# Gate projection of four token groups, in place of two, by seven block products

## The chip, the cores and the metric

The kernel runs on one core of one Trainium2 chip. The metric is the device time of one execution in microseconds (us), as the median of several executions. An engine is named as the profile names it: PE (TensorE, matrix products), DVE (VectorE), ACT (ScalarE), POOL (GpSimd) and SP (SyncE, which issues transfers). A bank is one of the eight parts of the matmul accumulator memory, 128 x 512 float32 each.

## The reference

Linear attention with cosine and sine weights, and behind it a gated feed-forward block. There are 8 batches with 8 heads of 576 positions of 64, which make 4608 tokens of 512; the hidden size is 1536.

```python
def phi(x, c, s):
    r = np.maximum(x, 0.0)
    return np.concatenate([r * c, r * s], axis=-1)
q_p = phi(q, cos_w, sin_w)
k_p = phi(k, cos_w, sin_w)
kv = np.einsum('bhsf,bhsd->bhfd', k_p, v)
z = np.sum(k_p, axis=2)
num = np.einsum('bhsf,bhfd->bhsd', q_p, kv)
den = np.einsum('bhsf,bhf->bhs', q_p, z)[..., None] + 1e-06
x = num / den                      # then heads side by side: (4608, 512)
...
g = x @ w_gate
silu = g * (1.0 / (1.0 + np.exp(-g)))
val = x @ w_val
return (silu * val @ w_out).astype(np.float32)
```

## The kernel before

**Groups and tiles.** The 4608 tokens are worked on in nine groups (0 to 8) of 512 tokens. A group has four tiles of 128 tokens. A tile comes out of the attention part as x (eight small matmuls on PE at line 435, then den, rec and x on DVE at lines 445, 454 and 458), and its transpose xT is made by a DMA transpose that SP issues (line 535). A batch has 576 tokens, so some tiles span two batches and take 16 matmuls.

**A group's feed-forward.** In the plain form (`ffn_fc`, line 571) a group takes twelve steps. In each, PE makes the gate and the value projection of 128 hidden columns, with four matmuls of 512 columns each (line 551); ACT takes silu of the gate (557) and DVE multiplies both into ht (562). Then the output projection follows (`out_by_quarters`, line 754, for groups 2 to 8), which already uses seven block products for eight; its operands are the weight differences T1 to T4 and the sums S1 to S4 of ht (line 747, `token_sum`).

**The seven-product form of the gate.** Groups in the tuple `GATE` use `ffn_by_quarters` (line 594) instead. The gate product of a third of the hidden columns (index u, three thirds) is seen as a 2 x 2 product of blocks: gate weights A11 to A22, tokens by depth B11 to B22. Seven products of four matmuls of 256 columns each (line 608) take the place of eight. The sums of weights W1 to W4 are made once (`gate_weight_sum`, 584), the differences of tokens X1 to X4 once for each group (`x_sum`, 592). Two intermediate results are copied by ACT (636 seeds bank b from bank a; 640 copies a product to m7), and two are added by DVE (646: c = m7 + b; 655: m7 = m7 + b) before four silus (614) read a, m7, c and b. The value projections V stay as they are (620), placed between the products, and the multiplication into ht is at line 625.

**The banks.** `take` (line 78) hands out banks by what was used longest ago. It prefers, for the banks of this form, a bank whose neighbour is in use, as long as fewer than three whole pairs are free, because a tile and a key-value product need a whole pair. In the first third of group 7 the second V is so given the bank that a had, which a silu has just read, and the third V the bank that c had.

**Order.** The program of each engine is in the order in which the lines are called. The dictionary `plan` holds what is done behind each step ("slot"): a group has 16 slots, twelve in its feed-forward (in the seven-product form the twelve calls of `done`) and four in its output projection. Into these slots go the tiles of the next group, the preparation of the next batch (q: relu on ACT at 253 and DVE products r_q at 270, DMA transposes phit at 293; k and v: relu at 253, DVE products at 274; key-value product on PE at 320 in slot 5 with its copies on ACT and DVE at 343), and the sums above. In groups 5 and 6 slots 0 to 2 hold three of the four k and v preparations of the next batch, and slot 5 its key-value product. Group 7 and 8 have neither.

**What depends on `GATE`.** Line 1021 spreads the four weight sums over slot 15 of groups between 1 and `GATE[0]`; line 1024 puts the four x differences of a group into slots 14 and 15 of the group before; line 1039 gives the slots of the tiles made in a group of `GATE`; lines 1044 to 1049 choose the form.

Of the kernel before, what the change touches and what calls it, by code (L numbers as in the profile page):

```python
# [18 lines left out]
def kernel(  # L19
# [29 lines left out]
    HT = T // 2  # L49
    HD = d_model // 2  # L50
    KH = KC // 2
    GATE = (7, 8)

    consts = ctx.enter_context(tc.tile_pool(name="consts", bufs=1))
    raw = ctx.enter_context(tc.tile_pool(name="raw", bufs=2))
# [515 lines left out]
    def ffn_fc(*a):  # L571

        ffn_mm(*a)
        ffn_act(*a)
# [6 lines left out]
    def gate_weight_sum(n):  # L581
        o, x, y, op = ((W1, A21, A22, ALU.add), (W2, W1, A11, ALU.subtract), (W3, A11, A21, ALU.subtract),
                       (W4, A12, W2, ALU.subtract))[n]
        nc.vector.tensor_tensor(out=o, in0=x, in1=y, op=op)
# [278 lines left out]
    def at(s, *fns):  # L863
        plan.setdefault(s, []).extend(fns)

    def slot(s):
        for f in plan.pop(s, ()):
            f()
# [151 lines left out]
    for n in range(4):  # L1020
        at(SLOTS * (1 + n * (GATE[0] - 1) // 4) + FC + 3, lambda n=n: gate_weight_sum(n))
    for tg in GATE:
        for n in range(4):
            at(SLOTS * (tg - 1) + FC + (2, 2, 3, 3)[n], lambda tg=tg, n=(2, 0, 1, 3)[n]: x_sum(tg, n))
    for t in range(2 * OUT, NTG * OUT):
# [9 lines left out]
        else:  # L1035
            if t in (13, 14, 15):
                s = SLOTS * 2 + t - 4
            elif tg - 1 in GATE:
                s = SLOTS * (tg - 1) + ((1, 2, 7, 9) if tg < 6 else (1, 2, 4, 7) if tg < 8 else (1, 2, 5, 6))[i]
            at(s, lambda t=t: a_tile2(t), turn(t))  # L1040
    for tg in range(1, NTG):
        s0 = SLOTS * tg
        if tg in GATE:
            ffn_by_quarters(tg, lambda i: slot(s0 + i))
        for fc in range(FC) if tg not in GATE else ():
            ffn_fc(tg, fc)
# [41 lines left out]
```

## Time and profile before

| | us |
|---|---|
| median of 3 executions | 326.43 |
| lowest, highest | 326.18, 327.39 |
| profiled execution | 327.39 |
| its span, first to last instruction | 325.6 |
| PE busy in the span | 310.1 (95%) |
| DVE busy | 228.7 (70%) |
| ACT busy | 143.8 (44%) |
| POOL busy | 35.7 (11%) |

The span is what the profile's clock covers; the profiled execution's own time has 1.8 us around it. The page divides the span into 40 slices of 8.1 us, and shows for each the share of time in which an engine was busy and the clock that PE was granted:

```profile
## 2 busy tenths in 40 slices
PE   8899999999999999999999999999999689997994
...
DVE  7864776787768977687678776967694358744672
...
PEclk9999999999999999999999999999999899999998
```

Each digit is in tenths, 9 being 90% or more. Groups 5 to 8 begin at 185.7, 218.1, 250.5 and 287.9 us, slices 22, 26, 30 and 35 (counted from 0). Durations of matmuls are shown with their pipeline, so one follows the next before its shown end; the distance of two starts is what a matmul costs when nothing waits.

### The profile page before, as it was taken

What the parts mean: (1) busy time and instruction counts of PE and PEld (TensorE: products, weight loads), DVE (VectorE), ACT (ScalarE), POOL (GpSimd) and SP (SyncE); (2) the same over time, 40 slices, a digit from 0 to 9 for tenths busy, and PEclk for the clock granted to TensorE, in tenths of its full rate; (3) what the DMA queues carried; (4) which work ended last, traced back from release to release, by engine and by line L of the source; (5) the groups of instructions that cost most, each with busy time, mean ns of one, the idle gap of its engine ahead of it and who ended that gap; (6) DMA issues with size and microseconds to landing.
All of it is one profiled execution on the core that took longest, in us unless ns stands there. A gap on an engine that the chain in (4) does not pass through costs nothing.

```text
span 325.6 us, 6776 instructions
## 1 busy us (share of the span) xinstructions
PE 310.1 (95%) x2696; PEld 190.4 (58%) x2696; DVE 228.7 (70%) x458; ACT 143.8 (44%) x264; POOL 35.7 (11%) x62
## 2 busy tenths in 40 slices
PE   8899999999999999999999999999999689997994
PEld 4596555454445674567456745674568456774573
DVE  7864776787768977687678776967694358744672
ACT  7563646653344365336533553365323234324431
POOL 7754102011002000200011002000000000000000
PEclk9999999999999999999999999999999899999998
DMA  7999999986996948894969895989512501040004
GB/s 261 216 200 197 206 192 157 205 104 111 196 185 86 201 73 167 101 197 87 176 95 161 143 167 90 183 116 173 88 34 47 116 16 32 3 115 16 0 2 129
DMA packets 74767, 41.07 MB, mean 126 GB/s; under 512 B 49904, under 2 KB 69872, under 8 KB 74736
## 3 DMA queue, kind: packets, MB, share of 16 engines
q1 hardware_dynamic: 51952, 22.55, 37.3%
q0 software_dynamic: 22192, 17.57, 36.1%
q10 hardware_dynamic: 592, 0.52, 0.5%
q8 instruction: 21, 0.34, 0.4%
q14 instruction: 10, 0.08, 0.1%
HBM read 37.75 MB, written 9.44 MB: 145 GB/s over the span
## 4 chain that ended last, share of the span: by engine, by line
PE 85%; DVE 8%; ACT 3%; DMA 2%; issue 1%; DVEq 0%; ACTq 0%
PE banks L551 44%; PE banks L773 16%; PE banks L716 6%; PE banks L620 6%; PE banks L608 4%; PE banks L320 3%; PE banks L435 2%; DMA xT<-x 2%; DVE ht L625 2%; ACT sg L614 2%; DVE sums L747 1%; DVE x L458 1%; PE banks L481 1%; PE banks L417 1%; DVE v L274 1%
## 5 line engine op out<-in xcount | busy, mean ns | idle before, releaser
L551 PE MATMUL banks<-xT,wg_sb 128*128 128x512 f16 (+2 forms) x368 | 86.6, 360 | 0.2 <-DMA xT<-x 0.2
L551 PE MATMUL banks<-xT,wv_sb 128*128 128x512 f16 (+2 forms) x368 | 86.6, 360 | 0.0
L557 ACT ACTIVATE sg<-banks 128x512 bf16<-128x512 f32 (+2 forms) x92 | 51.5, 560 | 76.2 <-PE banks L551 74.2
L562 DVE TENSOR_TENSOR ht<-sg,banks 128x512 f16<-128x512 bf16 (+2 forms) x92 | 57.9, 637 | 30.0 <-PE banks L551 22.8
L551 PEld LDWEIGHTS <-wv_sb 128*128 128x128 f16 x368 | 35.5, 98 | 37.4
L551 PEld LDWEIGHTS <-wg_sb 128*128 128x128 f16 x368 | 33.9, 98 | 31.8 <-issue 0.5
L773 PEld LDWEIGHTS <-ht 128*128 128x128 f16 x336 | 32.5, 98 | 4.2
L620 PE MATMUL banks<-xT,wv_sb 128*128 128x512 f16 x96 | 24.9, 386 | 8.4 <-ACT sg L614 7.1
L773 PEld LDWEIGHTS <-sums 128*128 128x128 f16 x252 | 24.5, 98 | 4.2 <-issue 0.8
L270 DVE TENSOR_TENSOR r_q<-raw_q,tab 128x1152 bf16<-128x1152 bf16 x24 | 17.6, 754 | 7.4 <-ACT raw_q L253 7.1
L716 PE MATMUL banks<-wo_sb,ht 128*128 128x512 f16 x96 | 22.7, 379 | 0.0
L458 DVE TENSOR_TENSOR x<-banks,rec 128x512 f16<-128x512 f32 (+1 forms) x32 | 21.6, 674 | 1.3 <-PE banks L417 0.3
L773 PE MATMUL banks<-wo_sb,ht 128*128 128x256 f16 x168 | 20.6, 273 | 0.0
L274 DVE TENSOR_TENSOR v<-raw_v,tab 128x1152 bf16<-128x1152 bf16 x27 | 19.9, 751 | 0.3 <-ACT raw_v L836 0.3
L773 PE MATMUL banks<-wt_sb,sums 128*128 128x256 f16 x168 | 19.8, 273 | 0.1
L773 PE MATMUL banks<-wt_sb,ht 128*128 128x256 f16 x168 | 19.5, 273 | 0.0
L620 PEld LDWEIGHTS <-wv_sb 128*128 128x128 f16 x96 | 9.4, 98 | 16.7 <-issue 10.3
L786 ACT ACTIVATE ob<-banks 128x512 f32<-128x512 f32 x14 | 8.4, 597 | 21.8 <-PE banks L773 21.8
L625 DVE TENSOR_TENSOR ht<-sg,banks 128x512 f16<-128x512 bf16 x24 | 15.6, 680 | 3.4 <-ACT sg L614 3.3
L253 ACT ACTIVATE raw_k<-raw_k 128x576 bf16<-128x576 bf16 (+1 forms) x25 | 17.0, 694 | 0.0
L614 ACT ACTIVATE sg<-banks 128x512 bf16<-128x512 f32 x18 | 10.3, 591 | 12.6 <-PE banks L608 12.5
L747 DVE TENSOR_TENSOR sums<-ht 128x1024 f16<-128x1024 f16 (+1 forms) x28 | 15.5, 553 | 0.4
(121 smaller groups left out, 333.3 us busy)
## 6 DMA issues: line engine op xcount, KB each, us to landing
out_dram<-ob SPq DMA_DIRECT2D x67, 128.0 KB, 2.4
raw_k<-in_k_dram POOLq DMA_DIRECT2D x7, 576.0 KB, 8.9
raw_q<-in_q_dram POOLq DMA_DIRECT2D x6, 576.0 KB, 6.1
raw_v<-in_v_dram POOLq DMA_DIRECT2D x6, 576.0 KB, 11.5
wo_sb<-in_moe_w_out_dram POOLq DMA_DIRECT2D x3, 512.0 KB, 12.8
wg_sb<-in_moe_w_gate_dram POOLq DMA_DIRECT2D x5, 256.0 KB, 9.0
wv_sb<-in_moe_w_val_dram POOLq DMA_DIRECT2D x5, 256.0 KB, 9.2
wo_sb<-in_v_dram SPq DMA_DIRECT2D x2, 576.0 KB, 4.2
```

The source lines that it names most:

```text
L253: nc.scalar.activation(out=out, in_=in_, func=AF.Relu)
L270: nc.vector.tensor_tensor(out=st[b, "q"][:, g], in0=o.unsqueeze(2).to_broadcast([P, NC, 2, D]), in1=tab, op=ALU.mult)
L274: nc.vector.tensor_tensor(out=v2s[b == 1][:, g, :, :, 0:D], in0=(first if b == 0 and g == 0 else {"v": raw_of(b, "v")})["v"][:, g].unsquee ...
L458: nc.vector.tensor_tensor(out=st["x", t].rearrange("p (y e d) -> p e y d", e=2, d=D)[:, :, ys], in0=ps[:, :, 0:2 * J * D1].rearrange("p e ...
L551: nc.tensor.matmul(out=st["f", tg, fc, lo][i], lhsT=(wg_sb, wv_sb)[i][:, kc, fs], rhs=xT[tg][:, ts, kc], start=(kc == 0), stop=(kc == KC - 1))
L557: nc.scalar.activation(out=sg[:, 0:n], in_=st["f", tg, fc, lo][0], func=AF.Silu, scale=DOWN)
L562: nc.vector.tensor_tensor(out=ht[:, fc, r:r + n], in0=st.pop(("s", tg, fc, lo))[:, 0:n], in1=ps[1], op=ALU.mult)
L620: nc.tensor.matmul(out=val[u, i, w], lhsT=wv_sb[:, kc, fc * P:(fc + 1) * P], rhs=xT[tg][:, :, kc], start=(kc == 0), stop=(kc == KC - 1))
L625: nc.vector.tensor_tensor(out=ht[:, fc], in0=gates[u, w][:, i], in1=val.pop((u, i, w)), op=ALU.mult)
L716: nc.tensor.matmul(out=o_ps[t], lhsT=ht[:, fc, r:r + P], rhs=wo_sb[:, fc], start=(fc == 0), stop=(fc == FC - 1))
L747: nc.vector.tensor_tensor(out=o[:, lo:hi], in0=x[:, lo:hi], in1=y[:, lo:hi], op=op)
L773: nc.tensor.matmul(out=to[i][:, 0] if len(to) == 2 else to[0][:, i], lhsT=a[:, kc, i * P:(i + 1) * P], rhs=b[:, kc], start=first and kc == ...
```

## The change

One tuple is changed:

```diff
-    GATE = (7, 8)
+    GATE = (5, 6, 7, 8)
```

By it, in the program:

- Groups 5 and 6 use `ffn_by_quarters` where they used `ffn_fc`. In each, 48 gate matmuls of 512 columns give way to 84 of 256. Six ACT copies (636, 640), six DVE additions (646, 655) and four x differences (592) are added; silus and multiplications stay twelve each, with silus over other tiles of the same size.
- The weight sums stand at the ends of groups 1, 2, 3 and 4, where they stood at the ends of 1, 2, 4 and 5. The last, W4, is so in slot 15 of group 4.
- The x differences of group 5 stand in slots 14 and 15 of group 4, those of group 6 in the same slots of group 5.
- The tiles of group 6 (made in group 5) and of group 7 (made in group 6) stand in slots 1, 2, 4 and 7, where they stood in 5, 7, 9 and 11. With each goes its transpose on SP's queue. The tiles of group 8 stay in 1, 2, 5 and 6 of group 7, those of group 5 in 5, 7, 9 and 11 of group 4.
- The sums S1 to S4 in groups 5 and 6 stand where `ffn_by_quarters` has them, in its last two thirds.

On PE, DVE, ACT and SP the order of groups 0 to 3 is the same but for the one weight sum, and that of groups 7 and 8 is the same.

## The prediction

> **What bounds the kernel now.** I read the page's chain of waits first:
>
> ```profile
> PE 85%; DVE 8%; ACT 3%; DMA 2%; issue 1%; DVEq 0%; ACTq 0%
> ```
>
> TensorE sets the end nearly everywhere, so a stage is worth what its TensorE stream takes. The change touches the feed-forward stages of groups 5 and 6. The view of busy time by window gives those two (now in the plain form, lines 551 to 563) and groups 7 and 8 (already in the seven-product form, lines 594 to 682). I set the bounds from the starts of the first gate matmul and of the first output matmul of each group:
>
> ```profile
> core 0: us, PE busy (x) PEld busy (x) DVE busy (x) ACT busy (x) POOL busy (x), PEclk, DMA share, GB/s
> 185.71:208.74 23.03, 23.03 (x201) 11.42 (x202) 18.06 (x34) 9.69 (x18) 2.41 (x4) 1.00 0.84 144
> 218.10:241.34 23.24, 23.24 (x210) 11.41 (x208) 18.55 (x35) 10.07 (x18) 0.00 (x0) 1.00 0.63 112
> 250.52:278.44 27.92, 23.09 (x166) 14.69 (x164) 17.49 (x35) 10.05 (x18) 0.00 (x0) 0.94 0.26 58
> 287.86:311.63 23.77, 20.16 (x134) 12.89 (x132) 13.73 (x23) 9.86 (x18) 0.00 (x0) 1.00 0.19 45
> ```
>
> Groups 5 and 6 have no TensorE idle at all. Groups 7 and 8 do, and they are longer, although they multiply less. The TensorE timeline of group 7 shows where (start, length, what; in brackets the idle time before it and what ended it):
>
> ```profile
> 252.70 0.60 PE L608 MATMUL banks<-xT,wg_sb 128*128 128x256 f16 x4
> 253.98 1.02 PE L620 MATMUL banks<-xT,wv_sb 128*128 128x512 f16 x4 [0.69 <-ACT sg L614]
> 254.84 0.42 PE L435 MATMUL banks<-kv,phit 128*128 128x65 bf16 x8
> 255.10 0.60 PE L608 MATMUL banks<-kvt,wgs_sb 128*128 128x256 f16 x4
> 255.54 0.60 PE L608 MATMUL banks<-kvt,wg_sb 128*128 128x256 f16 x4
> 258.22 1.67 PE L620 MATMUL banks<-xT,wv_sb 128*128 128x512 f16 x4 [2.09 <-ACT sg L614]
> 259.68 0.65 PE L435 MATMUL banks<-kv,phit 128*128 128x65 bf16 x8
> 260.14 1.04 PE L608 MATMUL banks<-xT,wgs_sb 128*128 128x256 f16 x4
> ...
> 271.94 1.02 PE L620 MATMUL banks<-xT,wv_sb 128*128 128x512 f16 x4 [0.49 <-DVE ht L625]
> ```
>
> A value projection (L620) waits for a silu, because it is given the bank that this silu reads: VectorE finishes the attention tile (L458), then the sum m7+b (L655, 256.43 to 257.03), then ScalarE takes two silus, and only then is the bank free. After 2.09 us of idle the same four matmuls take 1.67 for 1.02, at a granted clock of
>
> ```profile
> 258.20:262.00 3.80, 3.78 (x22) 2.33 (x22) 1.57 (x4) 0.60 (x1) 0.00 (x0) 0.55 0.03 7
> ```
>
> From 258.22 to 262.27 the stream does one projection, one tile and three products. At full clock these are 0.863+0.26+3x0.437=2.43 us; the low clock costs 4.05-2.43=1.6.
>
> The TensorE page of the Trainium skill ("TensorE: Matmul & The Clock Gate", section "Why this matters for your kernels") sets about 3 us without matmuls as the gap that lowers the clock. Here 2.09 us was enough; by the page's rule neither new group would see the low clock, and the forecast would be near 340. The same page ("A second HAM failure mode: psum-queue depth-cycling") warns of short idles between matmul groups that share banks, which speaks against the change. I follow the trace.
>
> **The change, part by part.**
>
> *Removed and added matmuls.* Per group 12 gate projections of four 512-column matmuls go; their pitch is 218.96-218.10=0.863, in all 10.36 us. In come 21 products of four 256-column matmuls at 250.96-250.52=0.437, in all 9.18. That is a gain of 1.18 per group if nothing waits.
>
> *What groups 7 and 8 made of it.* Group 7's stream without waits is 10.36 (value) + 9.18 + 4 tiles at 0.26 = 20.58; it took 27.92, so 7.3 us went to waits and low clock. Group 8, with no tiles, has 19.54 and took 23.77: 4.2 lost. The pool of banks hands out the same bank numbers in the first third of groups 5 and 6 as in group 7 (it depends only on the order of requests), so the same two projections wait for the same two silus. I therefore start from 27.92 for each, not from 23.77, and correct for what differs.
>
> *Operand sums at the group's start.* The four differences of x (L592) of group 5 go behind group 4's fourth r_q product, and the second pair also behind a v product and the weight sum W4, in VectorE's order. The VectorE timeline of the boundary between 5 and 6 shows the queue they enter, and then what the boundary between 6 and 7 looks like, where they stand today:
>
> ```profile
> 218.00 0.76 DVE L270 TENSOR_TENSOR r_q<-raw_q,tab 128x1152 bf16<-128x1152 bf16 x1 [1.26 <-ACT raw_q L253]
> 218.68 0.68 DVE L788 TENSOR_SCALAR ob<-banks 128x512 f32<-128x512 f32 x1
> 219.28 0.75 DVE L274 TENSOR_TENSOR v<-raw_v,tab 128x1152 bf16<-128x1152 bf16 x1
> 219.94 0.95 DVE L584 TENSOR_TENSOR wgs_sb<-wg_sb,wgs_sb 128x1536 f16<-128x1536 f16 x1
> ...
> 248.71 0.75 DVE L592 TENSOR_TENSOR kvt<-xT 128x512 f16<-128x512 f16 x2
> 250.72 0.69 DVE L788 TENSOR_SCALAR ob<-banks 128x512 f32<-128x512 f32 x1 [1.26 <-PE banks L773]
> 251.33 0.87 DVE L592 TENSOR_TENSOR kvt<-xT,kvt 128x512 f16<-128x512 f16 x2
> ```
>
> In group 5 (start 185.4; the last transposed tile lands about 185.5): L270 to 185.91, X3 and X1 to 186.6, L788 to 187.2, L274 to 187.9, L584 to 188.75, X2 at 189.1. The product with X2 stands 1.74 after the start in group 7 (252.26); here it starts at 189.15, 3.75 after. So it is 2.0 us late, and all behind it shifts, because the next waits are chains from this product on. In group 6 W4 is no longer in the way: L270 to 218.68, X3 and X1 to 219.4, L788 to 220.0, L274 to 220.65, X2 to 221.0, so 1.2 late. What is late next: L646 and the first silu, which free the next projection's bank.
>
> *The key-value product of the next batch.* It stands in group 5 and 6 and not in 7. TensorE: from 228.45 to the tile at 229.73, 1.28 us. Behind it VectorE waits for ScalarE's two copies and does its own (L343, 0.87) before the three ht products that free the banks which the last third's second product and projection take. Walking it on group 7's clock: kv ends 270.06, VectorE's copies 271.8, three L625 at 0.6 to 273.65, projection at 273.7 where group 7 has 271.94: 1.76 late, 1.28 of it TensorE's own. The tile moved to slot 7 adds 0.26 of TensorE here and puts den, rec and x (1.1) ahead of L646: about 0.4 more. Together 2.2. In group 6 this tile spans two batches, 0.47 for 0.26: 0.2 more.
>
> *At nothing.* The weight sum now at the end of group 3 (0.87) and the r_k relus (0.67 each on ScalarE) lie in VectorE and ScalarE idle of a stage that TensorE fills; without that cover one costs its own length. The other v products (0.67) stand where VectorE in group 7 idles 1.64 and 3.34 us. The x transposes of groups 6 and 7 are issued earlier on SP's queue, ahead of the output stores by more than today; the one wait that exists for such a transpose (group 5's start, 0.3 us) disappears into the late X2 or stays: bounds 0 and 0.3, and I take the gain of 0.3, since my start of 185.4 already uses it.
>
> *Unshown.* No row has seven-product groups with a key-value product and v products. Bounds per group: from group 8's losses, 23.77+1.28+1.04=26.1 (3.1 more than today), to the walk with a second low-clock stretch, 32.1+1.6=33.7 (10.7 more). I take the walk, as group 7 with its tiles in the same slots 1 and 2 is the nearest row.
>
> *Sum.* Group 5: 27.92+2.0+2.2=32.1, against 23.03: +9.1. Group 6: 27.92+1.2+2.2+0.2=31.5, against 23.24: +8.3. Less 0.3: +17.1. The profiled execution took 327.39 (span 325.6); the median is 326.43, 1.0 below. 326.4+17.1=343.5.
>
> **The rivals.**
>
> *A, group 8's size.* If the v products and the copies fall wholly into idle time and the clock stays up, group 5 takes 26.1 and group 6, with its longer tile, 26.3, both 3.1 more than today: 326.4+6.2-0.3=332.3, with a spread to 336 if half of the walk's late operands come on top. For it: group 8 lost only 4.2. Against: it has no tiles, and these stand ahead of L655.
>
> *B, the clock stays low longer.* TensorE will be idle for 0.5+1.45+0.7+2.1 us in the first 9 us of group 5, more than in group 7, so a second stretch per group, 1.6 to 4 each: 347 to 351. Against: 1.55 us of idle in group 8 left the clock at 1.00.
>
> *C, not slower.* The products of groups 5 and 6 run without waits: 20.58+1.28=21.9 and, with the longer tile, 22.1, so 1.2 less each, 324.1. It decides as soon as the waits of a group stay below 1.2 us. For it: TensorE is the bound and its work shrinks. Against: both groups that have the form lose 4.2 and 7.3, and VectorE has more ahead of the sums in 5 and 6.
>
> *D, no change that can be told.* The waits of each group come to about the 1.2 us that its fewer matmuls save, which gives 326.4. It lies between A and C, and no group in the trace is near it.
>
> **How the numbers follow.** The walk 0.70 (own range 338 to 347: without low clock in either group 3.2 less; with one stretch more, 1.6 more, and rounding), A 0.16, B 0.10, C 0.03, D 0.01. The predicted time is the walk's, 343.5. The range 333 to 348 leaves out the upper part of B, the lower edge of A, C and D, under 2 in 10. A difference of about 0.5% is what a measurement of this kernel can tell from no change. Faster is C, 0.03; the same is D and C's edge, 0.02; slower is the rest, 0.95.
>
> **What would show it.** In the profile after: feed-forward windows of groups 5 and 6 of about 32 and 31.5 us with 7 to 9 us of TensorE idle or low clock (wrong if below 27). The product with X2 in group 5 waits for VectorE's L592 for about 1.5 us, in group 6 about 0.7. The projection behind each group's first third waits over 1.5 us for L614. The projection after the key-value product waits for L625. The granted clock falls below 0.95 over both windows. L608 doubles to 336 matmuls. Groups 7 and 8 keep 27.9 and 23.8 to within one low-clock stretch. If groups 5 and 6 show no waits for L614, the assumption that group 7 is the pattern was wrong.

## The result, and the profile after

The changed kernel takes 343.61 us (343.25 to 344.28, four runs) against 326.38 in the same comparison, a ratio of 1.0524 (95% interval 1.0496 to 1.0551): slower by 17.2 us. The prediction was 343.5. The chain of waits of the changed kernel:

```profile
PE 80%; DVE 11%; ACT 6%; issue 2%; ACTq 0%; DVEq 0%
PE banks L551 31%; PE banks L773 18%; PE banks L620 11%; PE banks L608 7%; PE banks L716 6%; ACT sg L614 4%; DVE ht L625 3%; PE banks L435 2%; DVE x L458 2%; PE banks L320 2%; DVE m L655 1%; DVE v L274 1%; PE banks L481 1%; PE banks L417 1%; DVE kvt L592 1%
```

TensorE's part of the chain fell from 85% to 80%, while VectorE's rose from 8% to 11% and ScalarE's from 3% to 6%: the chain now leaves TensorE through the silus and VectorE's steps before them. Busy time by window, for the feed-forward stages of groups 5 and 6, then 7 and 8 (columns as before: window, length, busy time of each engine, granted clock, DMA share, GB/s):

```profile
185.15:216.89 31.74, 24.72 (x238) 15.58 (x236) 23.05 (x45) 13.21 (x24) 2.41 (x4) 0.95 0.85 144
...
226.39:257.39 31.00, 23.51 (x246) 14.80 (x244) 22.18 (x44) 13.12 (x24) 0.00 (x0) 1.00 0.52 90
...
266.70:294.99 28.29, 23.01 (x166) 14.55 (x164) 17.49 (x35) 10.05 (x18) 0.00 (x0) 0.94 0.26 57
304.29:328.07 23.78, 20.17 (x135) 12.88 (x132) 13.74 (x23) 9.87 (x18) 0.00 (x0) 1.00 0.19 45
```

Group 5 grew from 23.03 to 31.74 and group 6 from 23.24 to 31.00, together 16.5 us, the whole difference of the two spans (342.0-325.6=16.4). Group 7's 0.4 more and the two output stages' 0.27 more are met by an earlier start of group 5, 185.15 for 185.71. The medians differ by 17.2, since the profiled execution of before was 1.0 above its median and that of the changed kernel 0.2.

The TensorE timeline of group 5 after the change, in parts (start, length, what, idle time before it and what ended it):

```profile
189.01 0.61 PE L608 MATMUL banks<-kvt,wgs_sb 128*128 128x256 f16 x4 [1.35 <-DVE kvt L592]
189.46 0.60 PE L608 MATMUL banks<-xT,wg_sb 128*128 128x256 f16 x4
190.74 1.02 PE L620 MATMUL banks<-xT,wv_sb 128*128 128x512 f16 x4 [0.69 <-ACT sg L614]
...
194.98 1.02 PE L620 MATMUL banks<-xT,wv_sb 128*128 128x512 f16 x4 [2.09 <-ACT sg L614]
195.84 0.59 PE L435 MATMUL banks<-kv,phit 128*128 128x65 bf16 x8
196.25 1.04 PE L608 MATMUL banks<-xT,wgs_sb 128*128 128x256 f16 x4
197.08 1.06 PE L608 MATMUL banks<-xT,wg_sb 128*128 128x256 f16 x4
197.93 1.06 PE L608 MATMUL banks<-kvt,wgs_sb 128*128 128x256 f16 x4
199.44 1.02 PE L620 MATMUL banks<-xT,wv_sb 128*128 128x512 f16 x4 [0.45 <-DVE ht L625]
...
202.02 1.02 PE L620 MATMUL banks<-xT,wv_sb 128*128 128x512 f16 x4 [0.69 <-ACT sg L614]
...
208.70 0.60 PE L608 MATMUL banks<-kvt,wgs_sb 128*128 128x256 f16 x4 [0.64 <-DVE ht L625]
209.89 1.02 PE L620 MATMUL banks<-xT,wv_sb 128*128 128x512 f16 x4 [0.60 <-DVE ht L625]
```

The product with X2 waits for VectorE's x differences, then come the same two waits for a silu as in group 7, 0.69 and 2.09 us, and behind the second the three products at nearly twice their pitch (0.83 and 0.85 us from start to start for 0.44). The last two lines stand behind the next batch's key-value product and wait for ht products of VectorE.

### The profile page after: what moved, and what is told of

Read it like the earlier page. It is cut to its first block, busy times and chain, and to the rows that moved or that the text cites. A ratio compares the mean times of both kernels' runs of the same rounds, so it can differ in the third digit from the quotient of the medians.

```text
span 342.0 us, 6928 instructions
## 1 busy us (share of the span) xinstructions
PE 311.4 (91%) x2768; PEld 197.6 (58%) x2768; DVE 238.5 (70%) x478; ACT 149.9 (44%) x276; POOL 35.9 (10%) x62
## 4 chain that ended last, share of the span: by engine, by line
PE 80%; DVE 11%; ACT 6%; issue 2%; ACTq 0%; DVEq 0%
PE banks L551 31%; PE banks L773 18%; PE banks L620 11%; PE banks L608 7%; PE banks L716 6%; ACT sg L614 4%; DVE ht L625 3%; PE banks L435 2%; DVE x L458 2%; PE banks L320 2%; DVE m L655 1%; DVE v L274 1%; PE banks L481 1%; PE banks L417 1%; DVE kvt L592 1%
## 5 line engine op out<-in xcount | busy, mean ns | idle before, releaser
L620 PE MATMUL banks<-xT,wv_sb 128*128 128x512 f16 x192 | 49.4, 383 | 19.3 <-ACT sg L614 14.3
L551 PE MATMUL banks<-xT,wg_sb 128*128 128x512 f16 (+2 forms) x272 | 62.0, 354 | 0.0
L551 PE MATMUL banks<-xT,wv_sb 128*128 128x512 f16 (+2 forms) x272 | 62.0, 354 | 0.0
L557 ACT ACTIVATE sg<-banks 128x512 bf16<-128x512 f32 (+2 forms) x68 | 37.2, 547 | 53.4 <-PE banks L551 51.3
L562 DVE TENSOR_TENSOR ht<-sg,banks 128x512 f16<-128x512 bf16 (+2 forms) x68 | 41.5, 620 | 22.5 <-PE banks L551 15.5
L551 PEld LDWEIGHTS <-wv_sb 128*128 128x128 f16 x272 | 26.1, 98 | 26.1
L551 PEld LDWEIGHTS <-wg_sb 128*128 128x128 f16 x272 | 25.0, 98 | 21.8
L625 DVE TENSOR_TENSOR ht<-sg,banks 128x512 f16<-128x512 bf16 x48 | 31.1, 680 | 3.4 <-ACT sg L614 3.3
L614 ACT ACTIVATE sg<-banks 128x512 bf16<-128x512 f32 x36 | 20.8, 591 | 27.7 <-PE banks L608 27.6
L608 PE MATMUL banks<-kvt,wgs_sb 128*128 128x256 f16 x144 | 22.1, 277 | 4.1 <-DVE kvt L592 2.7
L608 PEld LDWEIGHTS <-wgs_sb 128*128 128x128 f16 x192 | 18.2, 100 | 13.0 <-issue 3.5
```

Of the source, the lines that this page charges most:

```text
L551: nc.tensor.matmul(out=st["f", tg, fc, lo][i], lhsT=(wg_sb, wv_sb)[i][:, kc, fs], rhs=xT[tg][:, ts, kc], start=(kc == 0), stop=(kc == KC - 1))
L557: nc.scalar.activation(out=sg[:, 0:n], in_=st["f", tg, fc, lo][0], func=AF.Silu, scale=DOWN)
L562: nc.vector.tensor_tensor(out=ht[:, fc, r:r + n], in0=st.pop(("s", tg, fc, lo))[:, 0:n], in1=ps[1], op=ALU.mult)
L608: nc.tensor.matmul(out=to[:, i], lhsT=a[:, c, 2 * u + i], rhs=x[:, :, c], start=first and i == 0 and c == 0, stop=c == KH - 1, skip_group_ ...
L614: nc.scalar.activation(out=gates[u, w][:, :, j * HT:(j + 1) * HT], in_=src, func=AF.Silu, scale=DOWN)
L620: nc.tensor.matmul(out=val[u, i, w], lhsT=wv_sb[:, kc, fc * P:(fc + 1) * P], rhs=xT[tg][:, :, kc], start=(kc == 0), stop=(kc == KC - 1))
```

## The experiments

Each is timed against the kernel before on its own chip. Ratios are to that, with their 95% intervals. The kernel before took 326.38 to 327.09 us on these chips, so a difference in us between runs on different chips is good to about 0.7 us.

**Without the form.** The kernel before with an empty tuple; no weight sums are made.

```diff
-    GATE = (7, 8)
+    GATE = ()
...
-    for n in range(4):
+    for n in range(4 if GATE else 0):
```

> All nine groups in the plain form: GATE is empty, no weight sums and no x differences. Theory (the form itself loses, by its waits): groups 7 and 8 fall to their matmuls' own time, 20.72+4x0.26=21.8 and 20.7 us, 6.2 and 3.1 less than in the kernel before: 326.4-9.2=317.2, between 316.5 and 318.5. Rival (the waits in groups 7 and 8 come from where these groups stand, at the end with tiles and output sums, and the form saves its 1.2 us in each): 326 to 329.

Measured: 317.96 us, 0.9724 (0.9705 to 0.9744). Groups 7 and 8 take what their matmuls take (columns as above):

```profile
250.51:272.26 21.75, 21.75 (x130) 10.41 (x128) 13.57 (x26) 7.17 (x12) 0.00 (x0) 1.00 0.28 62
281.49:302.30 20.81, 20.81 (x99) 9.46 (x97) 10.92 (x17) 7.17 (x12) 0.00 (x0) 1.00 0.22 51
```

TensorE is busy in all of both windows, so the waits came with the form, as the kernel before had it, and not with the place of these groups. By it that kernel had already lost 8.6 us.

**Group 5 alone plain again.**

```diff
-    GATE = (5, 6, 7, 8)
+    GATE = (6, 7, 8)
```

> The changed kernel with group 5 in the plain form again (groups 6, 7, 8 in the new one). Theory (each converted group pays on its own): group 5 falls from 31.7 to 23.0, and its start waits for the transpose again: 343.6-8.7+0.5=335.4, between 334.5 and 336.5. Rival (the first converted group pays for late operand sums, whichever it is): group 6 takes over part of it, 337 to 340.

Measured: 335.11 us, 1.0253 (1.0225 to 1.0281), 8.5 below the changed kernel. In its trace group 6's gate begins at 218.2 and its output at 249.04: 30.8 us, as against 31.00. Each group pays on its own.

**The choice of bank.**

```diff
-                                      (hold[0] == "o" or hold[0] in "gv" and whole < 3),
+                                      (hold[0] == "o" or hold[0] in "gv" and whole < 2),
```

> The changed kernel; a value or gate bank is taken next to a bank in use only when fewer than two whole pairs are free (it was three). The second and third value projection of a group then get banks that were read long before. Theory (the choice of bank makes the waits for silu): the waits of 0.7 and 2.1 us in the first third and 0.7 in the second go, as do the 0.7 and 1.6 of group 8, and with them the low clock: 3 to 4.5 us in each of four groups, 327 to 332. Rival (VectorE's chain tile, m7 sum, three ht products is as long as the wait and only shows up one step later): 339 to 343.

Measured: 322.17 us, 0.9854 (0.9835 to 0.9874): 21.4 us below the changed kernel, more than the theory asked, and faster than the kernel before with twice as many groups in the form. The windows of groups 5, 6, 7 and 8:

```profile
185.19:211.22 26.03, 22.84 (x238) 14.85 (x236) 22.89 (x45) 12.94 (x24) 2.41 (x4) 1.00 0.94 149
220.72:246.01 25.29, 23.06 (x247) 14.83 (x244) 22.02 (x44) 12.94 (x24) 0.00 (x0) 1.00 0.62 111
255.31:276.76 21.45, 21.02 (x166) 13.93 (x164) 17.43 (x35) 9.91 (x18) 0.00 (x0) 1.00 0.34 75
286.07:305.60 19.53, 19.53 (x135) 12.91 (x133) 13.65 (x23) 9.76 (x18) 0.00 (x0) 1.00 0.24 55
```

The four groups lost 5.7, 5.7, 6.8 and 4.3 us of their length, and the clock stands at 1.00 everywhere. Group 8 now runs at the 19.54 us that the prediction worked out as its stream without waits. The idle time ahead of the value projections, 19.3 us in the changed kernel (14.3 for silus, 5.0 for ht products), is gone. The rows of the changed kernel and of this run (busy time, mean ns of one, idle time before and what ended it):

```profile
L620 PE MATMUL banks<-xT,wv_sb 128*128 128x512 f16 x192 | 49.4, 383 | 19.3 <-ACT sg L614 14.3 <-DVE ht L625 5.0
...
L620 PE MATMUL banks<-xT,wv_sb 128*128 128x512 f16 x192 | 48.6, 379 | 0.0
L608 PE MATMUL banks<-kvt,wgs_sb 128*128 128x256 f16 x144 | 21.6, 272 | 5.8 <-DVE kvt L592 2.7 <-DVE x L458 1.7 <-DVE ht L625 1.3
```

VectorE's work has not become less, and the same chain of x, m7 and silus runs. In group 8 nobody on TensorE waits for its end any more. In groups 5 and 6 a part of the wait comes back one step later, as the rival said: a product waits 0.68 us for x and another 0.63 for ht. The expectation was too small because the waits for ht, one step later, went too: with an old bank the projection does not wait for that product either. The output stage behind group 8 grew by 0.9 us; the run on two groups, below, shows that wait.

**The sum ahead of the tile.**

```diff
             V(u, 0, 0) if u else V(u, 1, 0)
-            done()
             product(b, u, W1, X1, False)
             nc.vector.tensor_tensor(out=m7, in0=m7, in1=b, op=ALU.add)
             silu(u, 0, 1, m7)
+            done()
```

> The changed kernel; the product with X1, the sum m7+b and its silu are issued ahead of the slot's tile, not behind it. Nothing else changes. Theory (the tile's den, rec and x, 1.1 us on VectorE, stand ahead of the sum that ends in the freed bank): the wait of 2.1 us falls to about 1.0 in groups 5, 6 and 7: 343.6-3.3=340.3, between 339 and 341.5. Rival (the three ht products behind both are what counts, in any order): 343 to 344.

Measured: 341.54 us, 1.0447 (1.0427 to 1.0468), 2.1 less where 3.3 was expected. The second wait is 1.80 in group 5, 1.86 in group 6 and 1.29 in group 7, which is 0.29, 0.29 and 0.85 less, 1.4 us in all. Most of the rest comes with the clock, which was 1.00 in all executions of this run and 0.986 to 0.995 in those of the changed kernel: group 7 takes 4.30 us from the second wait to the next projection, where it took 5.31. Group 7's wait comes near what the theory said. In groups 5 and 6 the expectation's "nothing else changes" was wrong: the slot holds a relu of k too, and it moved with the tile. ScalarE's timeline in group 5 shows it between the two silus that have to be done before the bank is free:

```profile
193.19 0.63 ACT L614 ACTIVATE sg<-m 128x512 bf16<-128x512 f32 x1 [2.27 <-DVE m L654]
193.72 0.67 ACT L253 ACTIVATE raw_k<-raw_k 128x576 bf16<-128x576 bf16 x1
194.30 0.58 ACT L614 ACTIVATE sg<-banks 128x512 bf16<-128x512 f32 x1
```

**The two groups with the other bank choice.** The kernel before with the edit of the bank choice alone.

> The kernel before (the form in groups 7 and 8 only) with the other bank choice alone. Theory (with it the form pays where VectorE has room): group 7 takes 21.5 and group 8 19.5 us as in the run with four groups and this choice: 326.4-6.5-4.2=315.7, between 315 and 316.7, below the plain kernel's 318.0. Rival (the order of banks inherited from a plain group 6 is another one and brings waits back): 317 to 321.

Measured: 317.36 us, 0.9704 (0.9684 to 0.9724). The time lies in the rival's range, though by the ratio it is 316.7 from 326.4, the theory's upper end. The rival's mechanism is not seen: groups 7 and 8 take 21.44 and 19.53 us as the theory said. About 1 us comes back behind group 8: its second output product waits until VectorE's last ht product is done, which by the theory of a later run reads the bank that the product gets. The TensorE timeline there:

```profile
300.79 1.47 PE L773 MATMUL banks<-wo_sb,ht 128*128 128x256 f16 x12
303.06 2.78 PE L773 MATMUL banks<-wt_sb,sums 128*128 128x256 f16 x24 [0.79 <-DVE ht L625]
```

**Key-value copies off VectorE.**

```diff
-        for w, eng in enumerate((nc.scalar.copy, nc.vector.tensor_copy)):
+        for w, eng in enumerate((nc.scalar.copy, nc.scalar.copy if b > 5 else nc.vector.tensor_copy)):
```

> The changed kernel; the copies of the key-value products that are used in groups 5 and 6 are all done by ScalarE, none by VectorE. Theory (VectorE's copy, behind ScalarE's, holds up the three ht products that free two banks): the waits of 0.64 and 0.60 for ht shrink to about 0.4 together, 0.8 less in each of two groups: 342.0, between 341.4 and 342.6. Rival (the time goes to the key-value matmuls themselves, 1.28 us, and the wait comes back for the third silu): 343.2 to 344.

Measured: 341.88 us, 1.0465 (1.0432 to 1.0498), 1.7 below the changed kernel, as the theory said; but not all of it is the edit. In its trace the wait of 0.64 in group 5 is gone and the one of 0.60 is 0.71, and from the second third's first value projection to the last third's first it takes 7.18 and 7.19 us in groups 5 and 6 for 7.87: 0.7 for each group, 1.4 in all. The clock differs besides: the profiled execution (343.70 us, mean clock 0.99) had it low in groups 5 and 6, while the other three (341.71 to 341.96) had a mean clock of 1.00.

**No v products, with the other bank choice.** The products at line 274 are left out for batches 6 and 7.

```diff
-        steps += [lambda b=b, g=g: (relu_k(b, g, g + 1, keng), vmul(b, g)) for g in range(G)]
+        steps += [lambda b=b, g=g: (relu_k(b, g, g + 1, keng), vmul(b, g) if b < 6 else None) for g in range(G)]
```

> The changed kernel with the other bank choice, and without the products v x weights (0.67 us each, four in a batch) of batches 6 and 7, so the key-value products of these batches read the values of an earlier batch. Theory (once the bank choice is mended, VectorE is the bound in the first third of groups 5 and 6, where its queue stands full from 185.8 to 196.5): about 2 us less in each of the two, 322.2-4=318.2, between 317.3 and 319.3. Rival (what is left are delays of chains across engines, with VectorE's load beside them): 320.8 to 322.

Measured: 320.3 us, 0.9792 (0.9769 to 0.9814): 1.9 less, between theory and rival. Groups 5 and 6 took 25.00 and 24.28, so 1.0 each for 2.7 us of VectorE work. Of the 3.1 us that TensorE's timeline shows as waits in group 5 with the bank choice, 1.0 went with these products; TensorE still waits 0.45 and 0.68 for the x differences, 0.35 for x and 0.63 for ht in group 5.

**Three edits together.** The bank choice, the copies on ScalarE, and

```diff
-            at(SLOTS * (tg - 1) + FC + (2, 2, 3, 3)[n], lambda tg=tg, n=(2, 0, 1, 3)[n]: x_sum(tg, n))
+            at(SLOTS * (tg - 1) + FC + 2, lambda tg=tg, n=(2, 0, 1, 3)[n]: x_sum(tg, n))
```

> The changed kernel with three edits: the other bank choice, all four x differences of a group in slot 14 (ahead of the copy to C12, the v product and the weight sum), and the key-value copies of batches 6 and 7 on ScalarE. Theory (VectorE's work is the bound in the first third, so only the copies taken off it count): 322.2-1.8=320.4, between 319.8 and 321. Rival (the late x differences are a wait of their own, and add): 322.2-1.8-1.8=318.6, between 318 and 319.3.

Measured: 320.83 us, 0.9817 (0.9791 to 0.9842), in the theory's range. The wait for X2 is gone, and a wait for the next step in VectorE's queue stands in its place, as TensorE's timeline of group 5 shows (three lines with a wait):

```profile
186.48 0.60 PE L608 MATMUL banks<-kvt,wgs_sb 128*128 128x256 f16 x4 [0.45 <-DVE kvt L592]
191.14 0.60 PE L608 MATMUL banks<-kvt,wgs_sb 128*128 128x256 f16 x4 [1.21 <-DVE banks L646]
195.14 0.60 PE L608 MATMUL banks<-kvt,wgs_sb 128*128 128x256 f16 x4 [0.67 <-DVE x L458]
```

The 1.35 us that the product with X2 waited have become 1.21 us for the sum at line 646. VectorE is busy for 11.33 of the 11.54 us from 185.33 to 196.87, so its queue is full from the group's start, and the order of its items moved most of the wait and did not remove it.

**The versions beside each other.** Three kernels on one chip, five rounds: the plain one again; two groups with the bank choice, with a free choice of bank in the last output projection too, and with the sum S4 moved behind S1 and S2:

```diff
-                                      (hold[0] == "o" or hold[0] in "gv" and whole < 3),
+                                      (hold[0] == "o" and (len(hold) == 2 or hold[1] < 8) or hold[0] in "gv" and whole < 2),
...
-                token_sum(*((3, 0, 4) if u == 1 else (4, 0, 4)))
+                if u == 1:
+                    token_sum(3, 0, 4)
...
             token_sum(n, 4, 6)
+        token_sum(4, 0, 4)
         done()
```

and groups 6, 7 and 8 with the three edits of the run before.

> The plain kernel (no seven-product form of the gate) once more, on the same chip as the next two, so that they can be compared directly. Both theories: 0.9724 of the kernel before, as in the first run, so 317 to 318.5.

> The kernel before with the form in groups 7 and 8, the other bank choice for gate and value, free bank choice in the last output projection, and the sum S4 of ht moved behind S1 and S2 at a group's end. Theory (in the last group the second output product waits 0.79 us and its pipeline's refill for a bank that the last ht product reads): that wait goes, about 1.0 less than with the bank choice alone, a ratio of 0.9704-0.003=0.967 to the kernel before, 316 to 316.8, about 1.5 below plain. Rival (the end of VectorE's queue stays the bound and only another product waits): ratio 0.970, 317 to 317.6.

> The form in groups 6, 7 and 8 with all three edits of the mended kernel (bank choice, x differences in slot 14, key-value copies on ScalarE). Theory (a group that also prepares a batch has no room on VectorE; group 6 takes 24.4 in the mended kernel against 23.2 plain): 1.2 more than with groups 7 and 8 alone, ratio 0.974, 318.2 to 319. Rival (group 6 pays once group 5 before it is plain): at or below the two-group kernel, 316 to 317.5.

Measured: plain 317.99 us, 0.9725 (0.9709 to 0.974); two groups 316.24, 0.9672 (0.9658 to 0.9687); three groups 318.95, 0.9759 (0.9743 to 0.9775). The two-group version is the fastest of all and beats both kernels. It gained the 1.0 us that its theory gave over the bank choice alone, and the wait of 0.79 is gone from its trace; its two further edits were made together, so which of them did it stays open. The three-group version lacks them and keeps that wait, which is about 1.0 of the 2.7 us that it takes more. The form pays in groups 7 and 8, and still costs more than it saves in group 6 (24.46 us against 23.25 plain).

## Why the prediction was right

*Start from group 7, not from group 8's losses.* Right, and it carried the number. Both new groups show group 7's waits at the same two projections (0.69 and 2.09 in group 5, 0.74 and 2.15 in group 6). The cause given, the bank that the silu has just read, is shown by the run that changes only the choice of banks. What the prediction did not say is that this choice was a fault of the kernel before as well, worth 9.7 us there (327.09 to 317.36 in the run on two groups).

*Late x differences.* The product with X2 starts 3.86 us after group 5's start (189.01) and 2.98 after group 6's (229.37), where 3.75 and 2.95 were worked out. The price of 2.0 and 1.2 stands as the distance in time. As a cause it was told too simply: the run with the differences moved forward shows VectorE's full queue behind it.

*Key-value product and the moved tile.* In group 7 of the kernel before it takes 6.02 us from the second third's first value projection to the last third's first (265.92 to 271.94), here 7.87 in both groups (202.02 to 209.89 in group 5): 1.85 for the 1.76 predicted. The tile in slot 7 costs 0.50 and 0.63, for 0.4 and 0.6. That VectorE's copies are part of it, the run with the copies on ScalarE shows (0.7 per group).

*The low clock.* This is the term that was mis-sized. It was priced at 1.6 us a stretch from the pace of the matmuls alone, and it stood in both groups by the start from 27.92. Group 6 had no such stretch (granted clock 1.00, where a fall below 0.95 was foretold), although it idled for 2.15 us. Its TensorE timeline from that wait:

```profile
235.46 1.02 PE L620 MATMUL banks<-xT,wv_sb 128*128 128x512 f16 x4 [2.15 <-ACT sg L614]
...
239.75 1.02 PE L620 MATMUL banks<-xT,wv_sb 128*128 128x512 f16 x4 [1.70 <-DVE ht L625]
```

At full clock it waits 1.70 us for the ht products, at low clock in group 5 it waits 0.45. From one projection to the other it is 4.29 us at full clock, 4.46 in group 5, 5.12 in group 7 of the kernel before and 5.31 in group 7 of the changed one. The run with the copies on ScalarE has both kinds in one trace, groups 6 and 7 from projection to projection (clock 0.67 and 1.00):

```profile
236.02:241.12 5.10, 4.23 (x24) 2.59 (x24) 2.85 (x6) 2.19 (x4) 0.00 (x0) 0.67 1.01 156
275.20:279.49 4.29, 2.59 (x25) 1.81 (x25) 2.85 (x6) 1.67 (x3) 0.00 (x0) 1.00 0.16 31
```

So a stretch costs 0.2 to 1.0 us: VectorE's chain of x and three ht products, 2.85 us busy in each, covers the rest. What the sum carried with 27.92 was the 0.8 us of group 7's stretch (5.12 for 4.29); the 1.6 entered the ranges alone. With this the steps close: 27.92+2.12+1.85+0.50-0.66=31.73 for group 5, measured 31.74 (the last term is 4.46-5.12), and 27.92+1.24+1.85+0.63-0.83=30.81 for group 6, measured 31.00, with silu waits 0.05 or so longer at three places. The forecast for the two groups was 0.9 us too high; the 0.4 of group 7, which was taken as unchanged, and the 0.8 by which the medians differ more than the spans make up for it, so the agreement to 0.1 us is partly luck.

*At nothing.* The weight sum at group 3's end cost nothing that can be seen: group 4 begins at 152.53 for 152.72. The wait for the transpose at group 5's start is gone; the group starts 0.56 us earlier, where a gain of 0.3 was taken.

*The rivals.* Group 8's size (332.3) failed: group 5 took 5.6 us more than its 26.1. Of these 2.1 are the late X2, 2.6 the tiles, which stand ahead of the m7 sum and of the ht products (2.09 us for group 8's 1.55 at the second wait, then 4.46 for 2.17 to the next projection, of which 0.26 were priced), and 1.6 the waits behind the key-value product; the last third is 0.6 shorter than group 8's. A longer low clock did not happen. "Not slower" and "no change" asked for waits of at most about 1.2 us a group; there were 9.8 and 8.9 us, over streams of 21.9 and 22.1 without waits. Groups 7 and 8 reach that state once the banks are chosen otherwise.

The rule of the Trainium skill's TensorE page ("TensorE: Matmul & The Clock Gate", "Why this matters for your kernels"), about 3 us without matmuls as the limit, does not fit this case: gaps of 2.09 and 2.14 us were followed by a clock near half (0.50 and 0.55). The same page's "What's actually happening" says that the window in which the clock gate watches activity is free-running and does not reset when a kernel starts. What is seen here is in keeping with that and does not prove it: nearly the same wait was followed by a low clock in group 5 and not in group 6.

## What to carry to other kernels

When a pool hands out accumulator banks, look at who read the bank last: a rule that protects one consumer's pairs can tie the next matmul to the newest reader and make a chain across engines out of independent work. Before a form with fewer multiplications is spread to more stages, compare the stages that already have it with their own stream without waits; here both were over it by 4 and 7 us, and that was the thing to mend. In the groups that also prepare a batch the fewer matmuls paid in no run here (25.19 and 24.45 us with three edits together, for 23.03 and 23.24 plain). The waits that are left there are for VectorE, which also makes the sums that replace the matmuls; how much of them is its full queue and how much the order of the steps is only shown in part.

## What the runs showed of the hardware

The granted clock fell to about half behind idle gaps of 2.1 us, for some 3 us, and not every time. Of nine such gaps (2.09 to 2.15 us) in the traces of the kernel before, the changed kernel, and the runs with group 5 plain and with the copies on ScalarE, six were followed by it and three were not. Three windows of the changed kernel, each at or after such a gap, in groups 5, 6 and 7 (the clock is the third number from the end):

```profile
196.00:199.00 3.00, 2.99 (x21) 2.05 (x18) 2.46 (x6) 1.17 (x2) 0.00 (x0) 0.50 1.05 150
235.30:240.00 4.70, 2.84 (x26) 1.94 (x26) 2.85 (x6) 2.35 (x5) 0.00 (x0) 1.00 1.04 165
274.50:278.20 3.70, 3.68 (x22) 2.17 (x22) 1.27 (x4) 0.49 (x1) 0.00 (x0) 0.55 0.02 3
```

In the run with the sum ahead of the tile, gaps of 1.80 and 1.86 us left it at 1.00. The same kernel can go either way: with the copies on ScalarE three executions had a mean clock of 1.00 and took 341.71 to 341.96 us, and the profiled one, with two such stretches, 343.70.
